# Other free partitions for w2 and dw2, and w2's tile zeroed in eight pieces later on

## The chip, the cores and the metric

The kernel runs on one core of one Trainium2 chip. The metric is the device time of one execution in microseconds. Three runs before the change took 402.86, 400.16 and 401.1 us, so the median is 401.1. The profile comes from one more execution, of 400.45 us, whose span from the first to the last recorded instruction is 398.5 us; 1.95 us lie around the span.

## The reference

The program computes a gated mix and all its gradients:

```
g   = sigmoid((x * gate_w).sum(-1))                      # x: [1, 1, 640]
a   = attention(x @ wq; k_cache, v_cache) @ wo           # 32 heads, 4096 keys, 128 wide
h   = x_B @ w1 + b1                                      # F = 1728
act = h * tanh(softplus(h))
b   = act @ w2                                           # w2: [1728, 640]
out = g * a + (1 - g) * b
outputs: out and the gradients of x, k_cache, v_cache, wq, wo, w1, b1, w2, gate_w
```

All tensors are bf16. There is one query position, so nearly all bytes are the two caches, which are read once, and their two gradients, which are written once: 32 heads with four tensors of 1 MB. In this kernel `dw2` replaces `w2` in the same on-chip tile, row by row, and is stored from there.

## The kernel before

**Heads.** For each head the kernel loads K and V ([128 partitions, 32, 128], 1 MB each), transposes them on TensorE (PE, L530) into PSUM, copies the result out on ScalarE (ACT, L539), multiplies it by the query and by the gradient row (L553), does a softmax over all 4096 keys, and forms dV and dK as outer products on VectorE (DVE, L613). Both are stored as 1 MB tiles. Loads of heads up to four ahead and the stores are issued by SyncE (SP), in program order, one queue. The order in which instructions stand on each engine is that of the program, written by hand.

**The start.** SP issues K and V of heads 0 to 3, parts of wq and wo, and w1 (L148). The first pass over head 0 waits for a chain: transposes of K (L530), the query row (L230), its columns (L241, L250), the gate, then `dy_ps` (L728), a product that spreads the output gradient over 128 partitions. DVE scales `dy_ps` into `da_bc` (L729) and ACT into `db_bc` (L730). After that PE transposes the second half of K (L530) and wo (L343), and so on to the softmax of head 0 and its first outer product, whose store is the first DMA on SP's queue after w1.

**The gate** is `g_raw` (L713), one number on each partition, then four DVE instructions on 128x1 (L718 to L723) to `g_all` and `omg_all`, on which `da_bc` and `db_bc` wait.

**Small PSUM tiles** come from one pool, `grp`, with two buffers in turn. The order there is q_ps, z_ps, col_ps, pair_ps, two dy_ps, and then, before the change, do_ps (L282). A new tile waits until all readers of the tile two places before it have finished.

**w2.** The 1728 rows of w2 are taken as 108 rows of 16x640 (20 KB each), one row per partition, so 20 of 128 partitions are free. `SEG` says which partitions carry which rows. An indirect DMA from GpSimd (POOL, L196) loads them by row numbers that are held in `rowids`; a free partition's number lies above 107, and the DMA skips it (`bounds_check`). Because the free partitions of the tile must hold zeros, POOL zeroes partitions 0 to 63 of the whole tile first (L416). The load is issued after head 0's softmax (`row_ids`, L193, then L196), the store of dw2 at head 28 (L202). The row numbers are computed on DVE at the start (L185 to L189). `dx_parts`, used later for partial sums, serves as scratch there.

**The MLP steps** run in small portions between the heads (`mlp_some`). Three of them loop over `SEG`: the load of b1 (L418), the DMAs that move the row of h to partitions (L433), and the product on POOL that spreads dh (L497).

Of the kernel before, what the change touches and what calls it, by code (L numbers as in the profile page):

```python
# [8 lines left out]
ALU = mybir.AluOpType  # L9
AX = mybir.AxisListType  # L10
F32 = mybir.dt.float32
# [5 lines left out]
def kernel(  # L17
# [24 lines left out]
    nc = tc.nc  # L42
    P = 128
    _, H, Sk, Dh = A_k_cache.shape
    D = A_x.shape[-1]
    F = B_w1.shape[1]
# [4 lines left out]
    NG = H // G  # L51
    GD = G * Dh
    FCN = 16
    FP = F // FCN
    FW = 512
    FN = -(-F // FW)
    SEG = ((6, 10, 0), (20, 48, 4), (52, 128, 32))
    assert F == FP * FCN and F % 64 == 0 and SEG[-1][2] + SEG[-1][1] - SEG[-1][0] == FP
    assert SEG[0][2] == 0 and all(a[2] + a[1] - a[0] == b[2] for a, b in zip(SEG, SEG[1:]))
    scale = float(Dh) ** -0.5  # L60
    TB = 8
    NTB = J // TB
# [62 lines left out]
    def load_wo(g):  # L125
# [7 lines left out]
    mjunk = const.tile([P, F], BF16, name="mjunk")  # L133
# [16 lines left out]
    w2_flat = w2_sb[:].rearrange("p fc n -> p (fc n)")  # L150
# [3 lines left out]
    ident_bf = const.tile([P, P], BF16, name="ident_bf")  # L154
    nc.gpsimd.memset(ident_bf[:], 0.0)
    nc.gpsimd.affine_select(
        out=ident_bf[:], in_=ident_bf[:], compare_op=ALU.not_equal, fill=1.0,
        base=0, pattern=[[-1, P]], channel_multiplier=1,
# [16 lines left out]
    def grp(shape, dt, name):  # L175
        return grp_ps.tile(shape, dt, name=name, tag="grp")
# [3 lines left out]
    bT = const.tile([P, RC], F32, name="bT")  # L180
    dx_parts = const.tile([P, RC, NG + 3], F32, name="dx_parts")
    rowids = const.tile([P, 1], mybir.dt.int32, name="rowids")
    row_f = dx_parts[:].rearrange("p c k -> p (c k)")[:, 0:1]
    seg_f = dx_parts[:].rearrange("p c k -> p (c k)")[:, 1:1 + len(SEG)]
    nc.gpsimd.iota(rowids[:], pattern=[[0, 1]], base=2 * P, channel_multiplier=1)  # L185
    nc.vector.tensor_copy(row_f, rowids[:])
    for k, (a, b, i) in enumerate(SEG):
        nc.vector.reduce_sum(seg_f[:, k:k + 1], ident_bf[:, a:b], axis=AX.X)
        nc.vector.scalar_tensor_tensor(row_f, in0=seg_f[:, k:k + 1], scalar=float(i - a - 2 * P), in1=row_f,  # L189
                                       op0=ALU.mult, op1=ALU.add)  # L190

    def row_ids():
        nc.vector.tensor_copy(rowids[:], row_f)  # L193
# [44 lines left out]
    def col_mm(row):  # L238
        ps = grp([P, G], F32, "col_ps")
        for hh in range(G):  # L240
            nc.tensor.matmul(ps[:, hh:hh + 1], lhsT=row[0:1, hh * Dh:(hh + 1) * Dh], rhs=ones_bf[0:1, 0:1],  # L241
                             start=True, stop=True)
        col = small.tile([P, G], BF16, name="col", tag="col", bufs=2)
        nc.vector.tensor_copy(col[:], ps[:])
        return col
# [13 lines left out]
    def g_qcol(g):  # L259
        groups[g]["col"] = col_mm(groups[g]["q_row"])  # L260

    def g_qpair(g):
        groups[g]["pair"] = pair_mm(groups[g].pop("col"))
# [149 lines left out]
    dh_bf = const.tile([P, FCN], BF16, name="dh_bf")  # L413
    dh_bc = const.tile([P, F], BF16, name="dh_bc")
    nc.gpsimd.memset(h_sb[:], 0.0)
    nc.gpsimd.memset(w2_flat[0:P // 2, :].bitcast(F32), 0.0)  # L416
    for a, b, i in SEG:
        nc.gpsimd.dma_start(b1_sb[a:b, :], b1_v[i:i + b - a, :])  # L418
    mt = [const.tile([P, FCN], F32, name=f"mt{i}") for i in range(6)]

    def m_h(i):
# [7 lines left out]
        nc.scalar.copy(row, ps[:, 0:n])  # L429
        for a, b, i0 in SEG:  # L430
            lo, hi = max(i0, i * FW // FCN), min(i0 + b - a, (i * FW + n) // FCN)
# [101 lines left out]
    def ev():  # L533
        trq.pop(0)()
# [6 lines left out]
    def k_pe(h, c):  # L541
        if h < H:
            tr_pe(h, kts, KT, c)
# [143 lines left out]
    for c in range(2):  # L687
# [18 lines left out]
                                   op0=ALU.mult, op1=ALU.mult, accum_out=zp[:])  # L706
# [4 lines left out]
    g_raw = const.tile([P, 1], F32, name="g_raw")  # L711
    nc.vector.tensor_scalar(en[:], en[:], 1.0, None, ALU.add)
    nc.vector.reciprocal(g_raw[:], en[:])  # L713
    g_qcol(0)
    g_qpair(0)
    g_qpair_cp(0)
# [14 lines left out]
    da_col = const.tile([P, RC], BF16, name="da_col")  # L731
    nc.vector.tensor_scalar(da_col[:], dy_col_f, g_all[:], None, ALU.mult)

    for c in range(2, 4):
        k_pe(0, c)
        ev()
# [173 lines left out]
    for t in range(G):  # L910
# [19 lines left out]
                                   op1=ALU.add)  # L930
# [39 lines left out]
```

## Time and profile before

| what | us |
|---|---|
| median of three runs (400.16 to 402.86) | 401.1 |
| profiled execution, its time | 400.45 |
| its span | 398.5 |
| busy in the span: PE / DVE / ACT / POOL | 305.1 / 294.4 / 232.8 / 18.6 |
| HBM read / written | 82.44 MB / 82.44 MB, 414 GB/s over the span |
| SP's queue (q1), share of 16 DMA engines' time | 96.5% |
| POOL's queue (q0), share | 2.8% |

A timeline row gives the start in us from the span's start, the duration, the engine, the line and operation, the tiles, the shape, and in brackets for how long the engine was idle before it and what released it. A windows row gives, for a stretch of time, the busy time and the number of instructions on each engine, then the granted TensorE clock, the share of time in which the 16 DMA engines were busy, and the GB/s that they moved. The share can exceed 1 because the recorded times of two packets on one engine overlap a little.

### The profile page before, as it was taken

What the parts mean: (1) busy time and instruction counts of PE and PEld (TensorE: products, weight loads), DVE (VectorE), ACT (ScalarE), POOL (GpSimd) and SP (SyncE); (2) the same over time, 40 slices, a digit from 0 to 9 for tenths busy, and PEclk for the clock granted to TensorE, in tenths of its full rate; (3) what the DMA queues carried; (4) which work ended last, traced back from release to release, by engine and by line L of the source; (5) the groups of instructions that cost most, each with busy time, mean ns of one, the idle gap of its engine ahead of it and who ended that gap; (6) DMA issues with size and microseconds to landing.
All of it is one profiled execution on the core that took longest, in us unless ns stands there. A gap on an engine that the chain in (4) does not pass through costs nothing.

```text
span 398.5 us, 7712 instructions
## 1 busy us (share of the span) xinstructions
PE 305.1 (77%) x2933; PEld 206.1 (52%) x2949; DVE 294.4 (74%) x819; ACT 232.8 (58%) x468; POOL 18.6 (5%) x34
## 2 busy tenths in 40 slices
PE   2979979697898985885888977968797988677540
PEld 1556637464556663553565645645465645455320
DVE  8217728769696875778898986687898986669790
ACT  2466746654667663763566778575678756375320
POOL 8001010000000000000000030000000000010001
PEclk9999999968998998999898999879899899889855
DMA  7999999999999999999999999999999999999996
GB/s 271 424 416 409 401 425 421 424 420 424 423 426 424 422 417 423 426 415 427 424 423 425 422 424 421 426 412 423 427 423 426 423 424 421 423 435 404 406 417 251
DMA packets 28052, 164.55 MB, mean 413 GB/s; under 512 B 2967, under 2 KB 2968, under 8 KB 11416
## 3 DMA queue, kind: packets, MB, share of 16 engines
q1 hardware_dynamic: 27312, 159.62, 96.5%
q0 software_dynamic: 672, 4.44, 2.8%
q8 instruction: 23, 0.38, 0.4%
q14 instruction: 13, 0.11, 0.1%
q10 hardware_dynamic: 32, 0.01, 0.0%
HBM read 82.44 MB, written 82.44 MB: 414 GB/s over the span
## 4 chain that ended last, share of the span: by engine, by line
DMA 46%; DVE 28%; PE 17%; ACT 5%; issue 2%; POOL 0%; POOLq 0%; DVEq 0%; ACTq 0%
DMA out_dram<-o_sb 44%; DVE o_sb L613 10%; PE tr L530 7%; DVE junk L381 4%; DMA out_dram<-Vn 2%; DVE wq_p L391 2%; PE rw L553 2%; PE rw L646 2%; DVE mjunk L510 1%; DVE ident_f L165 1%; PE do_ps L282 1%; ACT do_row L285 1%; DVE Vn L613 1%; PE x L570 1%; ACT rw_sb L564 1%
## 5 line engine op out<-in xcount | busy, mean ns | idle before, releaser
L539 ACT COPY T<-tr 128x512 f32<-128x512 f32 x256 | 137.9, 595 | 54.6 <-PE tr L530 36.6
L613 DVE TENSOR_TENSOR o_sb<-qs_row,ds 128x2048 bf16<-128x2048 bf16 x58 | 70.7, 1218 | 35.5 <-DMA out_dram<-o_sb 35.5
L530 PE MATMUL tr<-ident_f,Vn 128*128 128x128 f32 x512 | 87.3, 306 | 6.8 <-ACT T L539 6.1
L530 PE MATMUL tr<-ident_f,Kn 128*128 128x128 f32 x512 | 85.7, 295 | 7.3 <-DVE ident_f L165 7.3
L530 PEld LDWEIGHTS tr<-ident_f,Vn 128*128 128x128 f32 x512 | 65.3, 158 | 27.9 <-PE tr L530 12.7
L530 PEld LDWEIGHTS tr<-ident_f,Kn 128*128 128x128 f32 x512 | 61.6, 150 | 23.8 <-PE rw L646 13.5
L613 DVE TENSOR_TENSOR o_sb<-do_row,p 128x2048 bf16<-128x2048 bf16 x58 | 69.8, 1246 | 0.0
L564 ACT COPY rw_sb<-rw 128x512 f32<-128x512 f32 x33 | 19.3, 586 | 49.1 <-PE rw L553 47.6
L646 PE MATMUL rw<-Kn,ds 128*4 128x512 bf16 x256 | 36.7, 413 | 3.5 <-DVE ds L608 3.2
L646 PE MATMUL rw<-Vn,p 128*4 128x512 bf16 x256 | 36.7, 413 | 0.0
L582 PE MATMUL mx<-ident_f,m_s 128*128 128x128 f32 x32 | 10.4, 325 | 27.5 <-DVE m_s L578 27.4
L570 PE MATMUL x<-ident_f,rw_sb 128*128 128x128 f32 x132 | 22.1, 291 | 4.6 <-ACT rw_sb L564 1.4
L381 DVE SCALAR_TENSOR_TENSOR junk<-wq_p,dq_bc 128x512 bf16<-128x512 bf16 x35 | 23.9, 684 | 0.0
L553 PE MATMUL rw<-T,qz 128*32 128x512 bf16 x256 | 22.5, 429 | 0.0
L598 PE MATMUL mx<-zd,ones_f 128*128 128x2 f32 x64 | 10.9, 241 | 14.2 <-DVE pj L594 14.0
L399 ACT ACTIVATE wo_g<-da_bc,o 128x640 bf16<-128x640 bf16 x28 | 20.9, 818 | 1.0 <-PE ax_ps L369 1.0
L553 PE MATMUL rw<-T,doz 128*32 128x512 bf16 x256 | 20.7, 400 | 0.8 <-ACT T L539 0.8
L590 ACT ACTIVATE e_bf<-x,negM 128x32 bf16<-128x32 f32 x32 | 9.4, 292 | 20.5 <-DVE dqo L654 20.3
L570 PEld LDWEIGHTS x<-ident_f,rw_sb 128*128 128x128 f32 x132 | 14.1, 143 | 13.5 <-ACT rw_sb L564 13.5
L582 PEld LDWEIGHTS mx<-ident_f,m_s 128*128 128x128 f32 x32 | 4.5, 141 | 32.0 <-DVE m_s L578 31.9
L646 PEld LDWEIGHTS <-ds 128*4 128x4 bf16 x256 | 9.3, 87 | 19.9 <-DVE ds L608 8.2
L598 PEld LDWEIGHTS mx<-zd,ones_f 128*128 128x128 f32 x64 | 10.5, 207 | 17.2 <-DVE pj L594 14.6
(177 smaller groups left out, 381.9 us busy)
## 6 DMA issues: line engine op xcount, KB each, us to landing
out_dram<-o_sb SPq DMA_DIRECT2D x58, 1024.0 KB, 16.2
Kn<-in_A_k_cache_dram SPq DMA_DIRECT2D x32, 1024.0 KB, 16.1
Vn<-in_A_v_cache_dram SPq DMA_DIRECT2D x32, 1024.0 KB, 17.7
wq_p<-in_A_wq_dram SPq DMA_DIRECT2D x4, 1280.0 KB, 14.2
wo_g<-in_A_wo_dram SPq DMA_DIRECT2D x8, 640.0 KB, 17.0
out_dram<-wo_g SPq DMA_DIRECT2D x8, 640.0 KB, 16.4
out_dram<-wq_p SPq DMA_DIRECT2D x4, 1280.0 KB, 10.9
out_dram<-Kn SPq DMA_DIRECT2D x3, 1024.0 KB, 10.0
```

The source lines that it names most:

```text
L381: nc.vector.scalar_tensor_tensor(jq[:], in0=wqs[g][:, c, :], scalar=1.0, in1=groups[g]["dq_bc"][:], op0=ALU.mult, op1=ALU.mult, accum_out= ...
L399: nc.scalar.activation(wos[g][:, hh, :], da_bc[:], ACT.Copy, scale=groups[g]["o4"][:, hh:hh + 1])
L530: nc.tensor.transpose(tp[:, t, :], words[:, t * P:(t + 1) * P], ident_f[:])
L539: nc.scalar.copy(T[h][:, (3 - c) * (TB // 2):(4 - c) * (TB // 2), :], tp[:])
L553: nc.tensor.matmul(rw[32 * c:32 * (c + 1), :], lhsT=z[:, par, :, :].rearrange("p m u -> p (m u)"), rhs=Tb[:, c, par, :, :], start=first an ...
L564: nc.scalar.copy(rw_sb[h][:].rearrange("p t r -> p (t r)"), rw[:])
L570: nc.tensor.transpose(xs[h][:, 3 - j, :], t[:, j, :], ident_f[:])
L582: nc.tensor.transpose(mx[:, 0:P], dgms.pop(h)[:].to_broadcast([P, P]), ident_f[:])
L590: nc.scalar.activation(es[h][:], sd[h][0], ACT.Exp, bias=negM[:], scale=scale, accum_out=zds[h][:, 0:1])
L598: nc.tensor.matmul(mx[:, P:P + 2], lhsT=ones_f[:], rhs=zds[h][:], start=True, stop=True)
L613: nc.vector.tensor_tensor(dst[:, a:b, :].rearrange("p j (k t) -> p j k t", t=4), row.rearrange("p (k t) -> p k t", t=4).unsqueeze(1).to_br ...
L646: nc.tensor.matmul(rw[32 * c:32 * c + 4, :], lhsT=c4[:, 4 * jb:4 * jb + 16].rearrange("p (j t) -> p t j", t=4)[:, 0, :], rhs=N[:, jb:jb + ...
```

## The change

The twenty free partitions become 3-4, 11-12, 16-19, 48-51, 67-68, 75-76, 83-84 and 91-92; before they were 0-5, 10-19 and 48-51. There are nine segments of used partitions in place of three. The row numbers are computed from a running count: a strictly triangular matrix `tri` (POOL), a column `keep` (DVE), and one small product on PE (`row_nos`) after the gate. The zeroing of w2's tile leaves the start: POOL copies `g_raw` to a scratch column, so that it waits for the gate, and then zeroes all 128 partitions in eight pieces of 128x640 f32 words.

```diff
-    SEG = ((6, 10, 0), (20, 48, 4), (52, 128, 32))
+    HOLES = ((3, 5), (11, 13), (16, 20), (48, 52), (67, 69), (75, 77), (83, 85), (91, 93))
+    SEG, at = [], 0
+    for a, b in zip((0,) + tuple(b for a, b in HOLES), tuple(a for a, b in HOLES) + (P,)):
+        SEG.append((a, b, at))
+        at += b - a
...
-    row_f = dx_parts[:].rearrange("p c k -> p (c k)")[:, 0:1]
-    seg_f = dx_parts[:].rearrange("p c k -> p (c k)")[:, 1:1 + len(SEG)]
-    nc.gpsimd.iota(rowids[:], pattern=[[0, 1]], base=2 * P, channel_multiplier=1)
-    nc.vector.tensor_copy(row_f, rowids[:])
-    for k, (a, b, i) in enumerate(SEG):
-        nc.vector.reduce_sum(seg_f[:, k:k + 1], ident_bf[:, a:b], axis=AX.X)
-        nc.vector.scalar_tensor_tensor(row_f, in0=seg_f[:, k:k + 1], scalar=float(i - a - 2 * P), in1=row_f,
-                                       op0=ALU.mult, op1=ALU.add)
+    sk = dx_parts[:].rearrange("p c k -> p (c k)")
+    row_f = sk[:, 0:1]
+    tri = mjunk[:, D:D + P]
+    keep = mjunk[:, D + P:D + P + 1]
+    nc.gpsimd.memset(tri, 1.0)
+    nc.gpsimd.affine_select(out=tri, in_=tri, compare_op=ALU.is_gt, fill=0.0, base=0, pattern=[[1, P]],
+                            channel_multiplier=-1)
+    for k, (a, b) in enumerate(HOLES):
+        nc.vector.reduce_sum(sk[:, 1 + k:2 + k], ident_bf[:, a:b], axis=AX.X)
+    nc.vector.reduce_sum(row_f, sk[:, 1:1 + len(HOLES)], axis=AX.X)
+    nc.vector.tensor_scalar(keep, row_f, -1.0, 1.0, ALU.mult, ALU.add)
+
+    def row_nos():
+        ps = grp([P, 1], F32, "row_ps")
+        nc.tensor.matmul(ps[:], lhsT=tri, rhs=keep, start=True, stop=True)
+        nc.vector.scalar_tensor_tensor(row_f, in0=row_f, scalar=float(2 * P), in1=ps[:], op0=ALU.mult, op1=ALU.add)
...
-    nc.gpsimd.memset(w2_flat[0:P // 2, :].bitcast(F32), 0.0)
...
     nc.vector.reciprocal(g_raw[:], en[:])
+    nc.gpsimd.tensor_copy(dx_parts[:, 0, NG + 2:NG + 3], g_raw[:])
+    for fc in range(0, FCN, 2):
+        nc.gpsimd.memset(w2_flat[:, fc * D:(fc + 2) * D].bitcast(F32), 0.0)
     g_qcol(0)
...
     nc.vector.tensor_scalar(da_col[:], dy_col_f, g_all[:], None, ALU.mult)
 
+    row_nos()
     for c in range(2, 4):
         k_pe(0, c)
```

More of the change, by code (lines that the diff above doesn't have):

```diff
@@ L56 @@
     FN = -(-F // FW)
-    SEG = ((6, 10, 0), (20, 48, 4), (52, 128, 32))
-    assert F == FP * FCN and F % 64 == 0 and SEG[-1][2] + SEG[-1][1] - SEG[-1][0] == FP
-    assert SEG[0][2] == 0 and all(a[2] + a[1] - a[0] == b[2] for a, b in zip(SEG, SEG[1:]))
+    HOLES = ((3, 5), (11, 13), (16, 20), (48, 52), (67, 69), (75, 77), (83, 85), (91, 93))
[3 more added lines that the diff above has]
+        at += b - a
+    assert F == FP * FCN and at == FP
     scale = float(Dh) ** -0.5
```

## The prediction

> **What bounds the kernel now.** I read the chain of waits first. DMA has the largest share of it, and the windows by stage show the 16 DMA engines full almost everywhere: from 10 to 390 us their share stays between 0.97 and 1.03 in every stretch of 10 us.
>
> ```profile
> DMA 46%; DVE 28%; PE 17%; ACT 5%; issue 2%; POOL 0%; POOLq 0%; DVEq 0%; ACTq 0%
> ...
> 0.00:2.00 2.00, 0.00 (x0) 0.00 (x0) 0.71 (x5) 0.00 (x0) 1.39 (x10) 1.00 0.06 17
> 2.00:4.00 2.00, 0.00 (x0) 0.00 (x0) 2.00 (x3) 1.28 (x1) 2.00 (x8) 1.00 0.84 295
> 4.00:6.00 2.00, 0.00 (x0) 0.00 (x0) 2.00 (x3) 0.00 (x0) 2.00 (x1) 1.00 0.98 381
> ...
> 34.00:36.00 2.00, 1.53 (x14) 1.29 (x13) 1.55 (x6) 1.15 (x3) 0.00 (x0) 1.00 1.17 457
> 36.00:38.00 2.00, 2.00 (x21) 1.30 (x19) 1.07 (x3) 1.36 (x5) 0.00 (x0) 1.00 0.95 392
> ...
> 390.00:392.00 2.00, 0.00 (x0) 0.00 (x0) 0.00 (x0) 0.00 (x0) 0.68 (x2) 0.50 1.00 396
> 392.00:394.00 2.00, 0.00 (x0) 0.00 (x0) 0.00 (x0) 0.00 (x0) 0.00 (x0) 0.50 0.77 295
> 394.00:396.00 2.00, 0.00 (x0) 0.00 (x0) 0.00 (x0) 0.00 (x0) 0.00 (x0) 0.50 0.51 200
> 396.00:398.00 2.00, 0.00 (x0) 0.00 (x0) 0.00 (x0) 0.00 (x0) 0.00 (x0) 0.50 0.12 49
> ```
>
> The last number but one is the DMA share. It is full from 4 us on, and it fades from 1.00 to 0.12 over the last 6 us: some DMA engines finish well before others. So an edit can move the end in two ways only. It can let the DMA engines run dry somewhere, or it can take work from the engines that finish last. Work saved on PE, DVE or ACT is worth nothing by itself.
>
> Then I read the timelines of the first 40 us, where POOL zeroes w2's tile.
>
> ```profile
> 1.55 0.28 DVE L163 TENSOR_REDUCE res<-ident_bf 128x4 f32<-128x128 bf16 x1
> 1.75 5.47 DVE L165 CAST ident_f<-ident_bf 128x128 f32<-128x128 bf16 x1
> ...
> 2.59 0.19 POOL L214 MEMSET ds<- 128x128 bf16 x1
> 2.73 0.10 POOL L415 MEMSET h_sb<- 128x16 f32 x1
> 2.78 4.35 POOL L416 MEMSET w_sb<- 64x5120 f32 x1
> ...
> 10.00 2.29 PE L230 MATMUL q_ps<-wq_p,cols_bf 128*128 128x512 bf16 x5 [0.64 <-DVE zj L705]
> 13.64 0.95 PE L728 MATMUL dy_ps<-mjunk,ones_bf 1*128 1x320 bf16 x2
> 14.52 1.97 PE L530 MATMUL tr<-ident_f,Kn 128*128 128x128 f32 x8
> ...
> 15.18 0.99 ACT L730 ACTIVATE db_bc<-dy_ps,omg_all 128x320 bf16<-128x320 f32 x2 [2.19 <-DVE da_bc L729]
> ...
> 33.65 0.35 SPq L631 DMA_DIRECT2D out_dram<-o_sb  x1
> ```
>
> DVE's cast L165 starts at 1.75 and ends at 7.22, 0.08 us after the memset L416: it was shut out for as long as POOL wrote. PE starts its query product at 10.00.
>
> **Part 1, the memset leaves the start: worth 0.** Without it the cast ends soon after POOL's small memsets, near 3.4 us. Added before it are a memset and a select of 128x128 (0.20 and 0.29 by L155 and L156) for an iota of 0.12. K of head 0 lands at 5.5 to 5.7 (the landings that the trace records for its DMA), so PE's first transposes start at about 5.7 and not at 7.28. But the next step, q_ps at 10.00, needs the part of wq whose last engine lands at 9.93. So the chain goes on where it did. DVE's row numbers become 10 small instructions in place of 7 (0.14 to 0.23 us each, L186 to L189), under the same wait. Nine b1 loads in place of three cost POOL 9 x 0.55 = 5 us, the ninth after the first has landed (5.6 us after issue), done before 10 us, while POOL's next work is at 13.4.
>
> **Part 2, the row product and its PSUM tile: +1.3 us on the start chain.** `row_ps` is a new tile in the two-buffer pool, straight after the two dy_ps. It takes the first dy_ps's place, so PE waits until DVE (L729, 15.15) and ACT (L730) have read that one. ACT's two take 0.99 together, so the first ends near 15.7. Queued behind on PE are the transposes that began at 14.52; now they begin near 15.8. Behind them stand ACT's copies, the softmax of head 0, the first store (33.65) and POOL's load of w2 (32.26): the chain of waits runs through them without a gap that could take this up. Bounds: 0.6 (if ACT's first alone ends at 15.1) and 2.5 (if PE, idle for 1.3 us, also runs these 8 transposes and the 20 after them at the slower of its own rates, 1.97 against 1.04 us for 8).
>
> What that does to DMA: before the first store the queue holds w1, which lands engine by engine from 35.1 to 37.1, median 35.66. The first packets of a load came 1.0 us after its issue (K of head 0: issued 0.75, first packet 1.76), those of w2 2.45 us (32.26 to 34.71). Shifted by 1.3 both come at 35.95 to 36.0. So the DMA engines stand dry for about 0.3 us (bounds 0 and 1.5), and as they are full from there to the end, this is paid once, in full: **+0.3**. Afterwards compute catches up, since SP issues 8 MB from 33.65 to 45.02, 20 us of DMA work at 424 GB/s.
>
> **Part 3, other rows on other DMA engines: -0.4.** Of a DMA of w2 the trace has 108 packets of 20480 bytes at 0.76 us and one landing for each of 16 engines: one at 35.5, two at 40.1 and 40.4, two at 41.9 and 42.2, eleven from 43.8 to 46.0. [...]
>
> [...] The last landings of the last big store are at 393.1 to 393.6 for eight engines and at 395.6 to 397.5 for eight; the latter are the bound. [...] The latest stands 0.4 ahead of the second, so -0.4 (bounds 0 and -1.5).
>
> **Part 4, hidden.** POOL's copy waits for g_raw (13.38); behind it on POOL stand only the eight memsets and w2's load, which is issued 14 us after they end. DVE's new scaling of row_ps waits for PE (15.8); behind it stands the column copy L244, due at 21.5. The twelve DMAs of h in place of five cost POOL 0.54 each; the last still goes out at 63.6 and lands at 68.4, and its reader L437 runs at 79.0. The nine products L497 in place of three add six starts of about 0.1 us to 3.38; DVE's outer products waited 1.7 us for them before, while DVE elsewhere waits 35.5 us in all for stores, and DMA was full there (1.01). If that cover were gone it would be 0.6.
>
> **Sum:** +0.3 - 0.4 on the profiled 400.45 is 400.4; the median of the three runs stands 0.65 higher, so **401.0**.
>
> **Rivals.**
>
> *DVE is shut out again, now in the chain.* POOL's memsets run from about 13.6 to 18.3 (5120 words at 4.35 us for the same length, plus eight starts). DVE's L718 to L723, casts and scalings of 128x1 that stand ahead of da_bc, fall into that time (13.97 on). The cast L165 of 128x128 waited through nine ends of POOL memsets that followed one another; if a 128x1 does likewise, omg_all comes at 18.9, ACT's db_bc ends near 19.5, and PE's transposes start near 19.6: 5.1 late. The first store then goes at 38.75, packets at 39.8, against a queue dry from 35.7: 4.1 us, less 0.4, is +3.7, so 404.8. It decides once a 128x1 is shut out at all. For it: the 5.47 us. Against it: no row has a 128x1 from on-chip memory beside a POOL memset, and the reductions L161 and L163 beside POOL's memsets took their 0.28.
>
> *The pieces let DVE in.* Then each of the four waits for at most one piece of 0.59, half of it on average, some 1.6 in all, and PE starts 1.6 later than in my sum: dry 1.9, +1.5 in all, 402.6. For it: DVE's scaling L606 at 231.38 got in at the end of one POOL product, after 0.4 us. Against it: the nine ends above. [...]
>
> [...]
>
> *The change does not do what it says*, because rows go to engines by their order and not by partition: the landings in groups of 1, 2, 2 and 11 speak against it; it would leave +0.3, 401.4, inside my own case.
>
> **Numbers.** Forecast (401.0) 0.45, DVE shut out (404.8) 0.27, pieces (402.6) 0.15, balance (399.6) 0.13. About 1% (4 us) is what a measurement of this kernel tells from no change; only the first rival with PE's slower rate on top (+1.5) passes it above, nothing passes it below but a mishap of the sum. So faster 0.04, same 0.82, slower 0.14. The range runs from 399.2 (balance, and 0.4 for the spread of medians) to 405.0.
>
> **What would show it.** L165 under 2 us long; q_ps still at 10.0; L718's successor row at its old 0.15 us or at 4 us; the transposes after dy_ps at 15.8 (19.6 for the rival); first store at 35.0; a DMA share below 0.9 in 34 to 40 us only for the rival; and last landings closer together than 393.1 to 397.5. I am wrong if the DMA share falls in a stage that this text doesn't name.

## The result, and the profile after

The changed kernel took 403.81 us (median of 7 runs) beside 401.43 for the kernel before: a ratio of 1.0051, 95% interval 1.0026 to 1.0075. Measured twice more, on two chips, it gave 1.0060 (1.0037 to 1.0082) and 1.0026 (1.0011 to 1.0041). All runs together: a median of 403.7 (31 runs) against 401.8 (137 runs). So it is slower by 0.3 to 0.6%, about 2 us, where the forecast was no change. The profiled execution took 404.03 us, its span is 402.3.

The chain of waits still has DMA first, in nearly the old shares:

```profile
DMA 46%; DVE 28%; PE 17%; ACT 4%; issue 2%; POOL 0%; POOLq 0%; SPq 0%; DVEq 0%; ACTq 0%
```

The timelines of the first 40 us of the changed kernel (start, duration, engine, line, operation, and in brackets the idle time before it; the line numbers of the changed file are 3 to 13 higher than the old ones):

```profile
1.81 1.59 DVE L168 CAST ident_f<-ident_bf 128x128 f32<-128x128 bf16 x1
...
5.85 1.94 PE L540 MATMUL tr<-ident_f,Kn 128*128 128x128 f32 x8 [5.85 <-DMA Kn<-in_A_k_cache_dram]
10.22 2.29 PE L241 MATMUL q_ps<-wq_p,cols_bf 128*128 128x512 bf16 x5 [2.31 <-DMA wq_p<-in_A_wq_dram]
13.78 4.63 POOL L726 MEMSET w_sb<- 128x640 f32 x8
14.75 0.15 DVE L736 CAST omg_all<-g_bf 128x1 f32<-128x1 bf16 x1
15.74 2.70 DVE L745 TENSOR_SCALAR da_col<-cols_f,g_all 128x5 bf16<-128x5 f32 x1
15.98 0.16 PE L200 MATMUL row_ps<-mjunk 128*128 128x1 bf16 x1 [1.17 <-ACT db_bc L743]
16.00 1.95 PE L540 MATMUL tr<-ident_f,Kn 128*128 128x128 f32 x8
16.18 2.27 DVE L201 SCALAR_TENSOR_TENSOR dx_parts<-dx_parts,row_ps 128x1 f32<-128x1 f32 x1
17.74 2.34 PE L354 MATMUL tr<-ident_bf,wo_g 128*128 128x128 bf16 x20
20.01 1.04 PE L563 MATMUL rw<-T,qz 128*32 128x512 bf16 x8
...
24.45 3.15 PE L540 MATMUL tr<-ident_f,Vn 128*128 128x128 f32 x16
...
37.36 0.35 SPq L641 DMA_DIRECT2D out_dram<-o_sb  x1
```

The cast is no longer shut out (1.59 us, 5.47 before). PE starts its first transposes 1.43 earlier, at 5.85, and then stands for 2.31 us, because the query product still waits for wq. Behind dy_ps PE stands for another 1.17 us until ACT has read the PSUM tile: the transposes begin at 16.00 (14.52 before). The first store, 33.65 before, goes at 37.36. From 17.74 on the same PE work also takes longer than in the kernel before, whose rows are:

```profile
16.28 1.82 PE L343 MATMUL tr<-ident_bf,wo_g 128*128 128x128 bf16 x20
18.04 0.64 PE L553 MATMUL rw<-T,qz 128*32 128x512 bf16 x8
...
21.79 2.03 PE L530 MATMUL tr<-ident_f,Vn 128*128 128x128 f32 x16
```

The windows by stage (busy time of PE, PE's weight loads, DVE, ACT and POOL, then the granted clock of PE, the DMA share and GB/s):

```profile
24.00:26.00 2.00, 1.75 (x16) 1.75 (x16) 0.43 (x3) 0.66 (x2) 0.00 (x0) 0.75 0.99 414
26.00:28.00 2.00, 1.60 (x8) 1.30 (x7) 0.00 (x0) 1.47 (x3) 0.00 (x0) 0.50 1.03 430
...
34.00:36.00 2.00, 2.00 (x28) 1.24 (x32) 1.84 (x6) 1.34 (x3) 0.05 (x1) 1.00 0.57 233
36.00:38.00 2.00, 1.89 (x23) 1.22 (x16) 2.00 (x3) 1.41 (x3) 1.16 (x1) 1.00 0.47 96
38.00:40.00 2.00, 1.52 (x14) 1.28 (x13) 1.55 (x6) 1.14 (x3) 0.00 (x0) 1.00 0.69 229
...
396.00:398.00 2.00, 0.00 (x0) 0.00 (x0) 0.00 (x0) 0.00 (x0) 0.00 (x0) 0.50 0.96 375
398.00:400.00 2.00, 0.00 (x0) 0.00 (x0) 0.00 (x0) 0.00 (x0) 0.00 (x0) 0.50 0.41 159
400.00:402.00 2.00, 0.00 (x0) 0.00 (x0) 0.00 (x0) 0.00 (x0) 0.00 (x0) 0.50 0.04 18
```

The clock column shows PE at half its clock from 25 to 28.4 us, where the kernel before had 1.00. (1.00 before the first record, at 21.6 us here and 17.4 before, means only that nothing is recorded: 8 transposes take 1.95 us there and 1.04 at the full clock. In a stretch that is recorded at half, from 78.9 us of the kernel before, four take 1.12, and 0.66 at full.) From 34 to 40 us the DMA engines run dry, and the end has moved by as much. Two wider rows for each kernel give the size. The kernel before:

```profile
30.00:40.00 10.00, 9.34 (x98) 6.16 (x100) 8.08 (x20) 6.69 (x15) 1.18 (x1) 1.00 1.03 411
40.00:50.00 10.00, 9.85 (x100) 6.62 (x97) 7.09 (x16) 7.20 (x15) 0.82 (x2) 1.00 1.00 401
```

The changed kernel:

```profile
30.00:40.00 10.00, 9.37 (x93) 6.99 (x92) 6.51 (x19) 6.68 (x15) 1.20 (x1) 1.00 0.75 276
40.00:50.00 10.00, 9.80 (x104) 6.58 (x102) 6.98 (x17) 7.01 (x17) 0.00 (x0) 1.00 0.98 373
```

135 and 28 GB/s less over 10 us each are 1.63 MB that were not moved. At the 424 GB/s of the full stretches that is 3.8 us of DMA work; the profiled time is 3.58 longer. So in this pair of traces the loss is all at the start. The trace of the kernel before is one of its faster executions, though (400.45; 112 of its 137 runs took more than 400.6), so the pair shows more than the 2 us between the medians.

### The profile page after: what moved, and what is told of

It is laid out like the page before. It is cut to its first block, busy times and chain, and to the rows that moved or that the text cites. A ratio compares the mean times of both kernels' runs of the same rounds, so it can differ in the third digit from the quotient of the medians.

```text
span 402.3 us, 7754 instructions
## 1 busy us (share of the span) xinstructions
PE 305.1 (76%) x2935; PEld 204.7 (51%) x2950; DVE 291.9 (73%) x823; ACT 233.4 (58%) x468; POOL 29.5 (7%) x62
## 4 chain that ended last, share of the span: by engine, by line
DMA 46%; DVE 28%; PE 17%; ACT 4%; issue 2%; POOL 0%; POOLq 0%; SPq 0%; DVEq 0%; ACTq 0%
DMA out_dram<-o_sb 44%; DVE o_sb L623 11%; PE tr L540 7%; DVE junk L392 3%; PE rw L563 2%; DMA wq_p<-in_A_wq_dram 2%; DVE wq_p L402 2%; DVE mjunk L520 2%; PE rw L656 2%; DVE Vn L623 1%; PE do_ps L293 1%; PE q_ps L241 1%; ACT do_row L296 1%; DVE ds L618 1%; DVE Kn L623 1%
## 5 line engine op out<-in xcount | busy, mean ns | idle before, releaser
L540 PE MATMUL tr<-ident_f,Vn 128*128 128x128 f32 x512 | 85.8, 302 | 7.7 <-ACT T L549 7.0
L540 PE MATMUL tr<-ident_f,Kn 128*128 128x128 f32 x512 | 84.3, 291 | 5.8 <-DMA Kn<-in_A_k_cache_dram 5.8
L540 PEld LDWEIGHTS tr<-ident_f,Kn 128*128 128x128 f32 x512 | 60.0, 147 | 23.7 <-PE rw L656 13.8
L563 PE MATMUL rw<-T,doz 128*32 128x512 bf16 x256 | 21.1, 406 | 0.7 <-ACT T L549 0.7
L507 POOL TENSOR_TENSOR mjunk<-ident_bf,dh_bf 128x96 bf16<-128x96 bf16 (+4 forms) x9 | 7.2, 833 | 166.2 <-issue 166.2
L608 PEld LDWEIGHTS mx<-zd,ones_f 128*128 128x128 f32 x64 | 10.3, 203 | 17.7 <-DVE pj L604 15.1
```

The costliest lines, as they stand in the source:

```text
L540: nc.tensor.transpose(tp[:, t, :], words[:, t * P:(t + 1) * P], ident_f[:])
L563: nc.tensor.matmul(rw[32 * c:32 * (c + 1), :], lhsT=z[:, par, :, :].rearrange("p m u -> p (m u)"), rhs=Tb[:, c, par, :, :], start=first an ...
L608: nc.tensor.matmul(mx[:, P:P + 2], lhsT=ones_f[:], rhs=zds[h][:], start=True, stop=True)
```

## The experiments

The theory: the start chain makes the first store late, DMA runs dry until it comes, and that is paid in full. It is late because of the wait for the PSUM tile (part 2) and because PE, standing twice, gets its full clock later. Rivals: the new rows of w2 cost the time (part 3), or the memset's new place (part 1), or a later chain through the heads. Sixteen runs tell them apart. The table has all medians, with the ratio to the kernel before on the same chip. The ratio is worked out from all runs of both and is not the quotient of the two medians. The runs that share a chip are e1 to e4; e5, e6, e7 and a1; e9, e10, e12 and e13; e11, e14, e15 and a2.

| run | edit | median us (runs) | before | ratio, 95% interval |
|---|---|---|---|---|
| a1 | changed kernel again | 404.11 (12) | 402.24 | 1.0060 (1.0037-1.0082) |
| a2 | and again | 402.48 (12) | 401.84 | 1.0026 (1.0011-1.0041) |
| e1 | changed, row product earlier | 400.85 (12) | 401.63 | 0.9993 (0.9967-1.0018) |
| e2 | before + part 1 | 402.88 (12) | 401.63 | 1.0024 (1.0004-1.0043) |
| e3 | before + wait of part 2 | 401.76 (12) | 401.63 | 1.0016 (0.9998-1.0034) |
| e4 | changed, old rows | 402.52 (12) | 401.63 | 1.0034 (1.0012-1.0056) |
| e15 | e4 again, beside a2 | 402.64 (12) | 401.84 | 1.0023 (1.0006-1.0040) |
| e5 | before + new rows | 402.45 (12) | 402.24 | 1.0027 (1.0000-1.0053) |
| e6 | changed, w2 loaded early | 401.30 (12) | 402.24 | 0.9976 (0.9954-0.9997) |
| e7 | changed, both PE gaps filled | 399.99 (12) | 402.24 | 0.9956 (0.9934-0.9979) |
| e9 | changed, first gap filled | 402.48 (12) | 401.86 | 1.0013 (0.9988-1.0037) |
| e10 | changed, second gap filled | 402.50 (12) | 401.86 | 1.0022 (1.0005-1.0040) |
| e12 | repaired, new rows | 400.28 (12) | 401.86 | 0.9966 (0.9951-0.9981) |
| e13 | repaired, old rows | 400.02 (8) | 401.86 | 0.9959 (0.9945-0.9973) |
| e14 | before, w2 loaded early | 400.18 (12) | 401.84 | 0.9964 (0.9949-0.9979) |
| e11 | repaired, even rows | 405.64 (6) | 401.84 | 1.0100 (1.0084-1.0116) |

Each run also left one trace. Beside its first store and its own time stand the bytes that its packets had moved by 50 us, as a loss against the trace of the kernel before (19.2 MB by then) at 424 GB/s:

| trace | first store us | lost by 50 us | profiled time | against 400.45 |
|---|---|---|---|---|
| before | 33.65 | 0 | 400.45 | 0 |
| e1 | 33.77 | 0.0 | 400.01 | -0.4 |
| e2 | 34.46 | 0.9 | 401.37 | +0.9 |
| e7 | 34.69 | 1.1 | 401.58 | +1.1 |
| e5 | 35.20 | 1.5 | 402.23 | +1.8 |
| e3 | 35.23 | 1.5 | 401.78 | +1.3 |
| a2 | 35.38 | 1.8 | 403.33 | +2.9 |
| a1 | 35.45 | 1.8 | 402.46 | +2.0 |
| e10 | 35.81 | 2.1 | 402.64 | +2.2 |
| e9 | 36.38 | 2.7 | 403.12 | +2.7 |
| e4 | 37.12 | 3.5 | 403.92 | +3.5 |
| e15 | 37.22 | 3.5 | 404.21 | +3.8 |
| after | 37.36 | 3.8 | 404.03 | +3.6 |
| w2 early: e6 | 35.05 | -0.9 | 401.65 | +1.2 |
| w2 early: e12 | 33.01 | -0.9 | 399.94 | -0.5 |
| w2 early: e13 | 35.41 | -0.7 | 400.70 | +0.3 |
| w2 early: e14 | 35.68 | -0.7 | 400.20 | -0.3 |
| w2 early: e11 | 33.25 | -0.8 | 405.62 | +5.2 |

Where w2 is loaded late, each us by which the store is late is about 1 us of DMA work lost and 1 us of time, from the smallest delay measured (0.8, e2) on. Of these only a2 lies off that line, by 1.1. Where w2 is loaded early, e13 took 1.0 and e6 about 2 us longer than its bytes say, and e11 6.0, of which more below. The DMA engines of a2 and e6 took 190.9 and 191.5 us for the bytes from 40 to 120 MB, against 189.3 (before), 189.5 (a1) and 189.8 (after); but those of e7, which lies on the line, took 190.5. Why stays open.

**What makes the store late.** e1 takes the row product out of dy_ps's way:

```diff
     g_new(0)
+    row_nos()
     g_q(0)
...
-    row_nos()
     for c in range(2, 4):
```

> Theory: the 2.4 us lost are the start chain. row_ps put ahead of the query product takes no slot of dy_ps, so PE's transposes follow dy_ps at about 14.5 again (16.00 in the changed kernel), the first store goes at 33.6 to 34.5 (37.36), and the DMA share from 34 to 40 us comes back above 0.9. Time: 403.8 less 2.5 to 3.5, so 400.3 to 401.3, at or below the kernel before. Rival, the new rows of w2 cost the time: the store moves the same way, but the time stays near 403.8. Rival, PE's clock alone (its idle 2.31 us before q_ps, which this run keeps): the transposes start at 14.5 but run at the slower rate, the store goes at 35.5 to 36 and the time is about 402.5.

The timeline of e1 has the transposes after dy_ps at 14.67, at the old rates behind them, and the store back:

```profile
10.15 2.29 PE L241 MATMUL q_ps<-wq_p,cols_bf 128*128 128x512 bf16 x5 [2.18 <-DMA wq_p<-in_A_wq_dram]
...
14.67 1.97 PE L540 MATMUL tr<-ident_f,Kn 128*128 128x128 f32 x8
16.43 1.81 PE L354 MATMUL tr<-ident_bf,wo_g 128*128 128x128 bf16 x20
...
33.77 0.35 SPq L641 DMA_DIRECT2D out_dram<-o_sb  x1
```

Store and time (400.85) came as the theory had them: the new rows, kept here, can't be the cause. e2 and e3 add one part each to the kernel before. e2:

```diff
-    nc.gpsimd.memset(w2_flat[0:P // 2, :].bitcast(F32), 0.0)
...
     nc.vector.reciprocal(g_raw[:], en[:])
+    nc.gpsimd.tensor_copy(dx_parts[:, 0, NG + 2:NG + 3], g_raw[:])
+    for fc in range(0, FCN, 2):
+        nc.gpsimd.memset(w2_flat[:, fc * D:(fc + 2) * D].bitcast(F32), 0.0)
```

> Part 1 alone: the kernel before, with the memset of w2's tile in eight pieces behind the gate. Theory: worth 0, q_ps at 10.0, transposes at 14.5, first store at 33.6 to 34, time 401.4 within 0.6. Rival (PE starts its first transposes at 5.9 and then idles 2.3 us, so its clock is granted in full later, 21.6 in place of 17.4 us): the first store 1 to 2 us later, DMA share below 0.9 somewhere from 34 to 40 us, time 402 to 403.

```profile
10.12 2.29 PE L230 MATMUL q_ps<-wq_p,cols_bf 128*128 128x512 bf16 x5 [2.14 <-DMA wq_p<-in_A_wq_dram]
...
16.39 2.34 PE L343 MATMUL tr<-ident_bf,wo_g 128*128 128x128 bf16 x20
...
34.46 0.35 SPq L630 DMA_DIRECT2D out_dram<-o_sb  x1
```

The rival's time came (402.88), with the store 0.8 us later and not 1 to 2. Transposes start at 14.63, as they should, but the 20 after them take 2.34 us: the records have the full clock from 19.1 us (17.4 before). Part 1 alone costs about 1 us (0.2 to 1.7). That PE's new gap is the reason is not shown: e1 has the same gap and the full clock from 17.5, and e14 below has no such gap and the full clock from 19.2. e3:

```diff
     da_col = const.tile([P, RC], BF16, name="da_col")
     nc.vector.tensor_scalar(da_col[:], dy_col_f, g_all[:], None, ALU.mult)
+    row_ps = grp([P, 1], F32, "row_ps")
+    nc.tensor.matmul(row_ps[:], lhsT=ident_bf[:], rhs=ones_bf[:, 0:1], start=True, stop=True)
+    nc.vector.scalar_tensor_tensor(dx_parts[:, 0, NG + 2:NG + 3], in0=row_f, scalar=float(2 * P), in1=row_ps[:],
+                                   op0=ALU.mult, op1=ALU.add)
```

> The wait of part 2 alone: the kernel before, with a product 128x1 in a PSUM tile of its own in the place of row_ps, and DVE's reading of it; holes and memset as before. Theory: PE waits for ACT's first db_bc, transposes at 15.8 to 16.0 in place of 14.52, first store 35 to 36.5, DMA share below 0.9 in 34 to 40 us, time 401.4 plus 1 to 2.5. Were the wait alone and at PE's old rates all, the store goes at 35.0 and the time is +0.3 to +1. Rival, the holes cost the time: 401.4 within 0.5, whatever the store does.

```profile
15.60 0.16 PE L735 MATMUL row_ps<-ones_bf,ident_bf 128*128 128x1 bf16 x1 [1.18 <-ACT db_bc L730]
15.62 1.95 PE L530 MATMUL tr<-ident_f,Kn 128*128 128x128 f32 x8
17.36 2.34 PE L343 MATMUL tr<-ident_bf,wo_g 128*128 128x128 bf16 x20
...
35.23 0.35 SPq L631 DMA_DIRECT2D out_dram<-o_sb  x1
```

The wait moves PE by 1.1 and the store by 1.58, and this trace lost 1.5 us of DMA work for it. Its median is only 0.13 above that of the kernel before (the ratio's interval: -0.1 to +1.4 us), less than the 1 to 2.5 expected. So either part alone is small, and neither alone makes the 2 us.

**Is it PE's clock?** a1 is the changed kernel once more.

> The changed kernel itself once more, with these three on one chip, so that they are compared with it directly. Theory (PE's clock is granted in windows of 3.4 us whose position against the start differs from run to run): times in two groups, near 402.3 and near 404.2, median 402.5 to 404, and in its profile the time of the first store goes with the time from which the clock is full. Rival, a fixed loss: all within 0.5 of 403.8 and the store at 37.4.

Its trace is that of the same program, and its PE begins the same work at the same time; in the rows shown only the clock differs:

```profile
15.96 1.95 PE L540 MATMUL tr<-ident_f,Kn 128*128 128x128 f32 x8
17.70 2.23 PE L354 MATMUL tr<-ident_bf,wo_g 128*128 128x128 bf16 x20
19.86 0.64 PE L563 MATMUL rw<-T,qz 128*32 128x512 bf16 x8
...
23.61 2.03 PE L540 MATMUL tr<-ident_f,Vn 128*128 128x128 f32 x16
...
35.45 0.35 SPq L641 DMA_DIRECT2D out_dram<-o_sb  x1
```

Its clock is full from 19.7 us to 81 without a break (21.6 in the first trace, then half from 25.0 to 28.4), its store goes 1.91 earlier, its time is 1.57 shorter. The 31 runs of this kernel fall into two groups: 12 from 401.8 to 402.8, 17 from 403.5 to 405.0, and two between. The five traces with this start (a1, a2, after, and e4 and e15 with the old rows) fit: where the clock is full from 19.7 or 19.8 on, they took 402.46 and 403.33; where it is full from 21.1 to 21.6 and half again about 3.4 us later, 403.92 to 404.21. e7 fills both stands of PE with products whose result is overwritten:

```diff
+    for _ in range(5):
+        nc.tensor.matmul(rw[:], lhsT=ident_bf[:], rhs=kts[0][:, 0:4, :].rearrange("p j d -> p (j d)"),
+                         start=True, stop=True)
     g_q(0)
...
+    for _ in range(3):
+        nc.tensor.matmul(rw[:], lhsT=ident_bf[:], rhs=kts[0][:, 0:4, :].rearrange("p j d -> p (j d)"),
+                         start=True, stop=True)
     row_nos()
```

> The changed kernel with 5 idle products of 128x512 put ahead of the query product and 3 ahead of row_ps, so that PE does not stand still in 7.9 to 10.2 and 14.8 to 16.0. Theory (idle PE delays the full clock): full clock granted from 17 to 18 us and no half clock at 25, transposes at 16.0 still, first store 35.2 in place of 37.4, time 403.8 less 1.5 to 2, so 401.8 to 402.3, with less spread between runs. Rival, the wait for the PSUM tile alone: clock and store as in the changed kernel, time 403.8 within 0.6.

It gave more than I expected: 399.99, 4.1 below a1 on the same chip (a2, on another, had 402.48), with the row product and its wait still there. In its trace the query product already runs partly at full clock, and of dy_ps's two products (0.95 us together before) each takes 0.30:

```profile
7.81 2.31 PE L713 MATMUL rw<-Kn,ident_bf 128*128 128x512 bf16 x5
10.10 1.99 PE L241 MATMUL q_ps<-wq_p,cols_bf 128*128 128x512 bf16 x5
...
13.42 0.30 PE L744 MATMUL dy_ps<-mjunk,ones_bf 1*128 1x320 bf16 x1
...
15.55 0.16 PE L200 MATMUL row_ps<-mjunk 128*128 128x1 bf16 x1 [0.56 <-ACT db_bc L746]
```

This trace is one of e7's longer runs (401.58): full from 11.7, half again from 15.1 to 18.5. The spread did not shrink (399.2 to 402.1). e9 keeps the first filling alone, e10 the second:

> Only the first of the two gaps of PE filled: 5 idle products of 128x512 between the first transposes and the query product (7.8 to 10.1 us); PE still stands from 14.7 to 15.9. Theory (the gap that part 1 opened by starting PE at 5.85 is what delays the full clock): most of what both fillings gave, 404.0 less 3 to 4, so 400 to 401. Rival (the gap before row_ps is the one): 403 to 404, as the changed kernel.

> Only the second gap filled: 3 idle products of 128x512 between dy_ps and row_ps; PE still stands from 7.9 to 10.2 us. Theory (the first gap counts): times in two groups as the changed kernel, median 402.5 to 404. Rival (the second gap counts): 400 to 401.

Both came to 402.5: e9 between its two expectations, e10 at the lower edge of its first. As a2, with nothing filled, has that median too on another chip, what each gap costs by itself is not shown. In e9's trace the clock, full from 10.4 us, is back at half from 13.9 to 20.7. The traces do show that filling the first gap brings the first stretch of full clock forward: it begins at 10.4 to 12.1 us in the five that have it (e7, e9, and e11 to e13 below), at 17.4 to 21.6 in the others. In all five a stretch of half clock follows.

**Is the dry queue the only way to the end?** e6 issues w2's load in the changed kernel right after the row product.

```diff
     row_nos()
+    row_ids()
+    w2_load()
...
-        if h == 0:
-            row_ids()
-            w2_load()
```

> The changed kernel with the load of w2 issued right after the row product (about 18 us) and not before the first store (36 us). Theory: the start chain reaches the time only through the dry DMA queue. The first store stays late (37 us, as the changed kernel), but 5 us of w2 lie in the queue before it, so the DMA share from 34 to 40 us is above 0.9 and the time falls by 2 to 3 to 400.8 to 401.8. Rival, the late heads themselves carry the loss to the end (a later chain, not DMA): time stays at 403 to 404 with the queue full.

It took 401.30, all 12 runs from 399.9 to 402.0, where 10 of a1's 12 on the same chip were above 403.7: 2.8 us are back, with row product, memset and new rows unchanged. (That the store would stay at 37 did not show: its one trace has 35.05, a good position of the clock.) e14 does the same to the kernel before, nothing else:

```diff
+    row_ids()
+    w2_load()
     da_col = const.tile([P, RC], BF16, name="da_col")
...
-        if h == 0:
-            row_ids()
-            w2_load()
```

> The kernel before with one change: row numbers cast and w2's load issued at 14 to 16 us in place of 32. Theory (the dry queue is the only way by which the start reaches the end, in the kernel before too): times of one group, 399.7 to 400.9, against 400.0 to 402.6 of the kernel before, whatever the clock does; DMA share full from 34 to 46 us. Rival (the early load costs w1 or the heads as much): 401.5 to 402.3.

400.18, eleven of 12 runs from 399.5 to 400.5. In its trace the clock is poor (full from 19.2, half from 22.6 to 26.0), and the first store goes at 35.68, 2 us later than that of the kernel before, although PE starts this work 0.2 earlier and neither part 1 nor part 2 is there. So the clock's position alone can make the store late, in the kernel before too:

```profile
16.09 2.34 PE L343 MATMUL tr<-ident_bf,wo_g 128*128 128x128 bf16 x20
18.36 1.02 PE L553 MATMUL rw<-T,qz 128*32 128x512 bf16 x8
```

But the DMA share stays at 0.97 and more:

```profile
34.00:36.00 2.00, 1.90 (x28) 1.02 (x17) 2.00 (x3) 1.02 (x3) 0.00 (x0) 1.00 0.97 401
36.00:38.00 2.00, 1.58 (x15) 1.34 (x14) 1.55 (x6) 1.21 (x4) 0.00 (x0) 1.00 1.01 406
38.00:40.00 2.00, 2.00 (x21) 1.33 (x19) 1.10 (x3) 1.36 (x5) 0.00 (x0) 1.00 1.03 411
```

Eleven of these 12 runs are shorter than 112 of the 137 of the kernel before, so most of its runs seem to pay the same price; these two lines moved beat it and the changed kernel.

**Do the new rows matter?** e5 put them into the kernel before, with its old way of numbering rows.

```diff
-    SEG = ((6, 10, 0), (20, 48, 4), (52, 128, 32))
+    SEG = ((0, 3, 0), (5, 11, 3), (13, 16, 9), (20, 48, 12), (52, 67, 40), (69, 75, 55), (77, 83, 61), (85, 91, 67),
+           (93, 128, 73))
...
-    nc.gpsimd.memset(w2_flat[0:P // 2, :].bitcast(F32), 0.0)
+    nc.gpsimd.memset(w2_flat[:, :].bitcast(F32), 0.0)
```

> Part 3 alone: the kernel before with the new free partitions of w2 and dw2, its memset at the start (over all 128 partitions), no row product. Theory: start chain as before (transposes at 14.5, first store 33.6 to 34.5), the early DMA engines of w2 gone but one, last landings about 1 us closer together, time 401.6 less 0.4 to 1.2, so 400.4 to 401.2. Rival, more descriptors of the pieces of b1, h and dh cost more than the balance gives: above 401.6.

402.45, above the 400.4 to 401.2 expected, but it doesn't tell what it was made for: nine segments mean 18 small DVE instructions in place of six, and its q_ps starts at 10.84, waiting for DVE. e4 takes the old free partitions in the changed kernel:

```diff
-    HOLES = ((3, 5), (11, 13), (16, 20), (48, 52), (67, 69), (75, 77), (83, 85), (91, 93))
+    HOLES = ((0, 6), (10, 20), (48, 52))
...
+        if a == b:
+            continue
```

> The changed kernel with the old free partitions of w2 and dw2, row product and memset pieces kept. Theory: first store as in the changed kernel (37.4), DMA share below 0.7 in 34 to 40 us, and without what the balance gives back: 403.8 plus 0.3 to 1, so 404.1 to 404.8. Rival, the new rows cost the time: about 401.4 again.

It was 402.52 where a1, on another chip, was 404.11, and so seemed to lean to the rival. Beside each other on one chip, a2 and e15 are equal (402.48 and 402.64):

> The changed kernel with the old free partitions, beside the changed kernel itself on one chip. Theory (the new rows are worth nothing either way): both medians within 0.7 of each other, in the same two groups (near 402.3 and near 404.1). Rival (the new rows cost time in this kernel): this one 1 to 2 lower, as the first comparison across two chips had it (402.5 against 403.8 to 404.1).

> The changed kernel beside its twin with the old rows. Theory: 403.5 to 404.2, twin within 0.7. Rival: twin 1 to 2 lower.

e12 and e13 compare the rows with the start repaired (e13 with e4's HOLES):

```diff
+    row_nos()
+    row_ids()
+    for _ in range(5):
+        nc.tensor.matmul(rw[:], lhsT=ident_bf[:], rhs=kts[0][:, 0:4, :].rearrange("p j d -> p (j d)"),
+                         start=True, stop=True)
     g_q(0)
...
+    w2_load()
     da_col = const.tile([P, RC], BF16, name="da_col")
...
-    row_nos()
...
-        if h == 0:
-            row_ids()
-            w2_load()
```

> The changed kernel with its start repaired in all three places: the row product ahead of the query product, the first gap of PE filled, w2's load issued at 14 to 18 us. Transposes at 14.4 to 14.7, first store at 33 to 34, DMA share full from 4 us to the end. What is left against the kernel before is the new rows alone. By part 3 (-0.4, bounds 0 and -1.5) and with the start better than before: 399.4 to 400.4. Rival (the balance is worth nothing): the same as its twin with the old rows within 0.4.

> The same with the old free partitions. By part 3 the time is 0.4 (0 to 1.5) above that twin: 399.8 to 401. Rival, the balance is worth nothing: equal within 0.4.

400.28 and 400.02: the kernel with the new rows is the longer by 0.26, and each ratio is known to about 0.6 us either way. So the balance, and the nine pieces of b1, h and dh with it, show no worth either way. Both are as fast as e14. e11 gives the repaired kernel free partitions that the author held to be better still; which DMA engine moves which rows, no run shows:

```diff
-    HOLES = ((3, 5), (11, 13), (16, 20), (48, 52), (67, 69), (75, 77), (83, 85), (91, 93))
+    HOLES = ((2, 6), (10, 14), (19, 21), (27, 29), (67, 69), (75, 77), (83, 85), (91, 93))
```

> [...] By part 3's reasoning the best balance there is: 0.4 or more below the twins (400.28 and 400.02), so at most 399.7. Rival (the balance is worth nothing): 399.8 to 400.5.

It was the worst of all: 405.64. The windows of its end:

```profile
394.00:396.00 2.00, 0.00 (x0) 0.00 (x0) 0.00 (x0) 0.00 (x0) 0.71 (x2) 0.50 1.05 402
396.00:398.00 2.00, 0.00 (x0) 0.00 (x0) 0.00 (x0) 0.00 (x0) 0.00 (x0) 0.50 0.53 200
398.00:400.00 2.00, 0.00 (x0) 0.00 (x0) 0.00 (x0) 0.00 (x0) 0.00 (x0) 0.50 0.07 25
400.00:402.00 2.00, 0.00 (x0) 0.00 (x0) 0.00 (x0) 0.00 (x0) 0.00 (x0) 0.50 0.07 28
```

A share of 0.07 is one engine of 16. The landings say the same: fifteen engines finish the last big store at 397.2 to 398.6, one at 402.9. The landings don't name their engine. The latest of the sixteen was 1.7 us behind the mean at 47.5 us, with a second close beside it, and then 2.5 at 136, 4.5 at 237 and 7.5 at 358. An earlier end of the other fifteen is no help while one ends 4.3 us after them.

## Why the prediction was wrong

*The reading.* "It can let the DMA engines run dry somewhere": that is what happened, in the stage that was named (34 to 40 us), and it is paid in full.

*Part 1, worth 0.* The cast (1.59), the transposes at 5.85 and q_ps (10.22) came as said. The 0 was wrong. Part 1 alone took about 1 us more (e2). PE stands there for 2.14 us ahead of q_ps (0.64 before), and the full clock came 1.7 later in that trace; that the one is the cause of the other stays open.

*Part 2 is the step that failed, in its size and not in its mechanism.* The wait is there: the product at 15.98 behind ACT's db_bc, transposes at 16.00 for 15.8. The sum made +0.3 of it, with bounds of 0 and 1.5; the kernels differ by about 2, and the changed kernel's traces lost 1.8 to 3.8. What was mis-sized is the slack: the text gave the queue 1.0 us, so that 1.3 late made 0.3 dry. There is none: the traces lose about 1 us of DMA work for each us of delay, already at 0.8 (e2). The median arrival of w1 was the wrong row to read: w2 and the stores bring their bytes later by the whole delay, and the rows from 30 to 50 us count them. a1 shows this best, as its first full clock has no break, like that of the trace before: its store is 1.8 later (the wait 1.3, q_ps 0.2), and it lost 1.8 us of DMA work and 2.0 of time. The slower rate of PE, which the text left as its outer bound (2.5), adds to that in some runs: of the 3.7 by which the store is late in the trace after, 2.2 are left for the clock. Not all of that is the change's, since e14 has such a clock without it. The share below 0.9 from 34 to 40 us, which the text kept for its first rival, came without that rival.

*Part 3, -0.4.* The new free partitions do change w2's landings: in the trace before, one engine lands at 35.5 us, two at 40.1 and 40.4, two at 41.9 and 42.2 and eleven from 43.8 on; in the trace after, one lands 8.3 us ahead of the mean and the fifteen others within 1.5 us of one another. Which partitions share an engine the landings don't show, and no run shows the -0.4 or its bound of -1.5: that the engines which end last get less to move was the author's estimate. In its place the runs show no gain (e12 and e13, a2 and e15): the last landings do lie closer, 3.1 to 4.0 us apart in the changed kernel's three traces and 4.3 in that of the kernel before, but the latest stands 1.7 to 2.7 behind the mean, and 2.4 before.

*Part 4, hidden.* Nothing speaks against it; POOL's longer work was tried only together with the new rows (e12 beside e13).

*The rivals.* DVE was not shut out where it matters: its four 128x1 steps beside the memsets kept 0.15 to 0.16 us (L736 above). da_col (0.22 before) and the scaling of row_ps were, for 2.70 and 2.27 us, but da_col's reader comes at 20.99. Nor did the pieces let DVE in: the 2.70 us are longer than four of the eight pieces (4.63 for all), and end with the last. The balance did not pay (400.28 with the new rows, 400.02 with the old). "Slower" was priced on the one mechanism and not on the chain's own clock.

What stays open: the share of each of PE's two gaps (e9, e10), and how much of the clock's lateness is the change's; why e1, with the first gap in it, did not lose e2's 1 us (their intervals overlap); and what holds up the one DMA engine.

## What to carry to other kernels

Where a kernel is bound by DMA from its first microseconds on, price each delay of the first store at its full length (here about 1 us of time for each us) unless a row shows bytes still queued behind it, and put a load whose place is free (here w2) there: here that made the start's delays harmless (e14: store at 35.68, 400.18 us). Starting an engine earlier on work that must wait later wasn't free here (e2, about 1 us), and neither was a small product in a shared PSUM pool (PE waited 1.17 us); look for the first place with no readers ahead. Take two traces of each kernel before an increment of 2 us is read from one pair.

## What the runs showed of the hardware

In the traces PE's granted clock changes in steps of 3.41 us, and where these lie against the start differs from run to run. All of its recorded stretches are multiples of that (61.4, 54.6, 6.8, 3.4; only the last is not), and the first full one began at 10.4 to 21.6 us in the traces of this study, at 19.7, 19.8 and 21.6 in three of the same kernel. The 1.57 us between two runs of one program, a1 (full from 19.7 us) and after (from 21.6), are nearly as much as this whole change.

POOL's memsets held up DVE's scaling of 128x5 (2.70 us, 0.22 before) and, queued behind it, that of row_ps (2.27 us), but not the casts and scalings of 128x1 (0.15 us).

In e11 the latest of the sixteen landings falls behind their mean by about 2 us in 100 (1.7 at 47.5 us, 7.5 at 358) and ends 5.2 behind it. As the landings don't name engines, that it is one engine all along is inferred. In the trace after, one engine is 5.2 us ahead of the mean at 52 us, and none more than 1.4 at 236. e11 is the only run here with rows of w2 on partitions 16 to 18 and 48 to 51; whether they are that engine's is not shown. The 23 packets of 16 KB in the instruction queue, at about 1.0 us each, are one candidate for what holds it up; no run tried it.
